# Decay attention in shares of 64 tokens: every product but the transposes as a 64x64 tile of TensorE

## The chip, the cores and the metric

One core of one Trainium2 chip runs the kernel. TensorE (PE) multiplies, and its weight loads are shown as an engine of their own (PEld); VectorE (DVE), ScalarE (ACT) and GpSimd (POOL) do the elementwise work; SyncE (SP) issues the DMAs. The metric is the device time of one launch in microseconds, the median of three runs.

## The reference

Two stages in a row. First a linear attention with decay: batch 4, 8 heads, 768 tokens, head width 64. Then a feed-forward block with softplus over all 3072 tokens, 512 to 2048 to 512 wide.

```python
gamma = 1.0 - 2.0 ** (-5.0 - np.arange(H))
for t in range(S):
    state = gamma * state + einsum('bhd,bhe->bhde', k[:, :, t], v[:, :, t])
    y[:, :, t] = (1 / sqrt(D)) * einsum('bhd,bhde->bhe', q[:, :, t], state)
x = y.transpose(0, 2, 1, 3).reshape(B * S, H * D)
h = x @ w_in                       # weights come as 64-bit floats
out = softplus(h) @ w_out
```

## The kernel before, in words

**Chunks.** The attention works on chunks of C = 128 tokens, 6 for each batch, 24 in all; `unit(m, first, pairs, when)` does chunk `m` for 8 heads (4 pairs), or, for the very first chunk, for 4 heads twice. q and v are multiplied by powers of gamma on load (`scaled`), so that a chunk needs only (1) the transposes of k and q (`tk`, `tq`, 4 each, 128x128), (2) the scores k.q of the chunk (`scores`), (3) a triangle set to zero (`mask`, an affine select of GpSimd over 128x1024 values), (4) y from the state at the start of the chunk and from the masked scores (`outputs`), and (5) the addition of the chunk's sum of k times v to the state (`update`). The state lies in `TD`, two heads to a tile, each padded with zeros to 128 rows.

**Shapes of the products.** All attention products are of full 32-bit floats, and each shows as two MATMUL records in the trace. Scores have 64 rows and 128 columns of weights, the two heads of a pair in the upper and lower half of the array (line 430). State and score shares of y have 128 rows and 64 columns of weights, 128 moving columns (lines 447 and 449). k times v has the same tile, 64 moving columns (line 453). All of them appear in the trace under line 322, the helper `mm`, with tile names by their banks: `a<-kt` is scores, `a<-ah,vn` and `a<-kt,td` are y, `a<-vn,kn` is the state. In the first chunks, buffers are lent from the weights' slots, so that `wout` or `win` stands for kt, ah or kn there. Transposes are line 417.

**The feed-forward block** runs in 6 blocks of T = 512 tokens with 16 steps each (`ffn_step`): 12 matmuls into a bank `hp` (`hp<-x,win`), softplus and a split into a rounded part `gh` and a rest `gl` on DVE, ACT and POOL (lines 515 to 519), and 12 matmuls into four banks `acc`. x itself is kept as such a pair, `xh` on ACT and `xl` on DVE (lines 461 and 462). These matmuls have 128x128 weights, 512 moving columns and one record each. During the first block the weights are fetched as 64-bit floats and turned into such pairs, too (`convert_weights`, lines 346 to 370).

**What sets the order.** All work is written down as operations with an engine, a cost, what they wait for and a due time (`when`), and `Planner.order` puts each engine's operations in one fixed order by those costs. `change` and the tables `ENTER` and `LEAVE` are the planner's prices for moving between the tile shapes R128 (feed-forward), T128 (transposes), S128 (scores) and V64 (y and state). Engines and DMA queues then run this order strictly. At the start of the program `ORDER` says which chunks and which half-width feed-forward steps (h0, h1: 256 tokens) come first; after that, chunks are added as the feed-forward steps go on, with `LEAD` and `STAGE` between due times.

## Time and profile before

| | before |
|---|---|
| median of 3 runs | 652.82 us (652.73 to 653.45) |
| the profiled execution | 651.83 us, its span 649.8 us |
| PE busy | 637.8 us (98%), 3928 matmul records |
| DVE, ACT, POOL busy | 256.9, 214.9, 239.8 us (40%, 33%, 37%) |
| TensorE's granted clock | 0.999 |

The span runs from the first to the last instruction; the execution's time has some 2 us more around it. PE's records overlap, and the end of each is modelled, so lengths of PE work are read here from the start of one row to the start of a later one.

### The profile page before, as it was taken

The page shows a single profiled execution, that of the slowest core. Times are in us where ns is not written, and L with a number is a line of the kernel's source. Part 1 is how long each engine was busy: PE and PEld are TensorE (multiplying, and loading weights), DVE is VectorE, ACT ScalarE, POOL GpSimd, SP SyncE. Part 2 cuts the span into 40 slices and gives each one's busy share as a digit, 9 for nine tenths or more (in the row PEclk, how much of TensorE's full clock was granted, in tenths as well). Part 3 has the DMA queues.
Part 4 walks back from the last instruction along what each step waited for, and adds up shares of the span by engine and source line. Part 5 has one row for each costly group of instructions (what it writes and reads, how often), then busy time and mean ns, then how long its engine had stood idle before and what let it go on. Part 6 is the DMA issues. An engine that isn't in the chain of part 4 may idle for free.

```text
span 649.8 us, 9615 instructions
## 1 busy us (share of the span) xinstructions
PE 637.8 (98%) x3928; PEld 524.7 (81%) x3928; DVE 256.9 (40%) x411; ACT 214.9 (33%) x360; POOL 239.8 (37%) x209
## 2 busy tenths in 40 slices
PE   6899999999999999999999999999999999999997
PEld 5788878888888888888888888887888888888886
DVE  5887888333232233323333324223332332322222
ACT  3776677222131222222222223122222222312221
POOL 4776777342332332232324232333223231212321
PEclk9999999999999999999999999999999999999999
DMA  9994664131102103201013201110310000100001
GB/s 230 279 310 127 212 211 125 35 80 50 33 19 53 28 17 97 49 17 33 17 32 82 66 17 30 36 33 18 98 44 5 1 1 1 65 1 0 1 1 65
DMA packets 89628, 42.58 MB, mean 66 GB/s; under 512 B 76272, under 2 KB 84464, under 8 KB 89584
## 3 DMA queue, kind: packets, MB, share of 16 engines
q1 hardware_dynamic: 89136, 41.95, 23.8%
q8 instruction: 31, 0.51, 0.3%
q14 instruction: 13, 0.11, 0.0%
q10 hardware_dynamic: 448, 0.01, 0.0%
HBM read 35.66 MB, written 6.29 MB: 65 GB/s over the span
## 4 chain that ended last, share of the span: by engine, by line
PE 97%; DMA 2%; ACT 0%; DVE 0%; issue 0%
PE acc L322 42%; PE hp L322 41%; PE a L322 11%; PE a L417 3%; DMA kn<-in_k_dram 1%; PE acc L417 0%; DMA qn<-in_q_dram 0%; ACT kt L423 0%; ACT w L554 0%; DVE qn L399 0%
## 5 line engine op out<-in xcount | busy, mean ns | idle before, releaser
L322 PE MATMUL hp<-x,win 128*128 128x512 f32 (+1 forms) x1176 | 285.3, 389 | 1.9 <-ACT x L461 1.4
L322 PEld LDWEIGHTS hp<-x,win 128*128 128x128 f32 x1176 | 214.7, 188 | 46.3 <-ACT x L461 1.5
L519 POOL TENSOR_TENSOR gl<-sp,gh 128x512 fp32r<-128x512 f32 x90 | 116.0, 1289 | 242.6 <-ACT gh L518 126.5
L322 PE MATMUL acc<-wout,gh 128*128 128x512 f32 x736 | 190.2, 394 | 0.0
L515 DVE TENSOR_SCALAR sp<-hp 128x512 uint32<-128x512 uint32 x92 | 63.6, 691 | 255.6 <-PE hp L322 172.4
L322 PEld LDWEIGHTS acc<-wout,gh 128*128 128x128 f32 x736 | 136.1, 188 | 29.7 <-issue 0.5
L516 ACT ACTIVATE sp<-sp 128x512 f32<-128x512 f32 x92 | 58.1, 631 | 271.8 <-DVE sp L515 271.6
L322 PE MATMUL acc<-wout,gl 128*128 128x512 f32 x368 | 104.7, 392 | 0.0
L517 DVE SCALAR_TENSOR_TENSOR sp<-hp,sp 128x512 f32<-128x512 f32 x92 | 63.4, 689 | 43.8 <-ACT sp L516 43.6
L322 PEld LDWEIGHTS acc<-wout,gl 128*128 128x128 f32 x368 | 68.5, 188 | 14.7 <-issue 0.2
L518 ACT CAST gh<-sp 128x512 fp32r<-128x512 f32 x90 | 55.8, 620 | 50.8 <-DVE sp L517 49.5
L399 POOL TENSOR_TENSOR vn<-vn,tabs 128x512 f32<-128x512 f32 (+1 forms) x24 | 24.2, 1009 | 57.4 <-DMA vn<-in_v_dram 57.4
L438 POOL TENSOR_SCALAR_AFFINE_SELECT ah<-ah 128x1024 f32<-128x1024 f32 x22 | 24.1, 1095 | 45.8 <-ACT ah L434 44.8
L322 PE MATMUL a<-ah,vn 128*64 128x128 f32 x352 | 33.7, 278 | 0.0
L399 POOL TENSOR_TENSOR qn<-qn,tabs 128x512 f32<-128x512 f32 x22 | 23.0, 1044 | 17.6 <-DMA qn<-in_q_dram 17.5
L322 PE MATMUL a<-kt,td 128*64 128x128 f32 x288 | 28.9, 279 | 0.0
L322 PEld LDWEIGHTS a<-kt 64*128 64x128 f32 x328 | 20.4, 187 | 7.2 <-issue 6.3
L322 PE MATMUL a<-kt 64*128 64x128 f32 x328 | 24.4, 285 | 0.0
L322 PEld LDWEIGHTS a<-ah,vn 128*64 128x64 f32 x352 | 22.4, 139 | 1.8 <-issue 0.7
L370 POOL TENSOR_TENSOR wout<-w,wout 128x512 fp32r<-128x512 f32 x16 | 20.7, 1292 | 7.2 <-ACT wout L369 7.0
L370 POOL TENSOR_TENSOR win<-w,win 128x512 fp32r<-128x512 f32 x16 | 20.7, 1291 | 6.8 <-ACT win L369 6.7
L346 ACT ACTIVATE raw<-raw 128x512 f32<-128x512 f32 x32 | 21.6, 677 | 2.9 <-DMA raw<-in_moe_w_in_dram 1.5
(99 smaller groups left out, 378.8 us busy)
## 6 DMA issues: line engine op xcount, KB each, us to landing
raw<-in_moe_w_in_dram SPq DMA_DIRECT2D x16, 512.0 KB, 6.2
raw<-in_moe_w_out_dram SPq DMA_DIRECT2D x16, 512.0 KB, 6.6
qn<-in_q_dram SPq DMA_DIRECT2D x22, 256.0 KB, 3.0
kn<-in_k_dram SPq DMA_DIRECT2D x22, 256.0 KB, 3.3
vn<-in_v_dram SPq DMA_DIRECT2D x22, 256.0 KB, 3.8
out_dram<-w SPq DMA_DIRECT2D x22, 256.0 KB, 2.6
out_dram<-win SPq DMA_DIRECT2D x2, 256.0 KB, 2.5
qn<-in_q_dram SPq DMA_DIRECT2D x2, 128.0 KB, 2.8
```

What stands on the lines that cost most here:

```text
L322: mm = lambda o, l, r, start, stop: emit(nc.tensor.matmul(o, lhsT=l, rhs=r, start=start, stop=stop))
L346: a = ACT(685, lambda word=word: emit(nc.scalar.activation(word(1).bitcast(F32), word(1).bitcast(F32), AF.Copy, scale=2.0**-112)), [ld], [ ...
L370: low_ = POOL(1300, lambda nm=nm, w=w: emit(nc.gpsimd.tensor_tensor(hl(nm, f)[:, 1], buf(w), hl(nm, f)[:, 0].bitcast(F32), op=ALU.subtract ...
L399: emit(engine.tensor_tensor(heads(held), heads(held), tabs[:, c, tab, hs].unsqueeze(2).broadcast_to([P, 2 * pairs, D]), op=ALU.mult))
L417: emit(nc.tensor.transpose(columns(tp[s], C)[:, j], heads(held)[:, 2 * j:2 * j + 2, :], ident))
L438: mask = [POOL(640 * 2, lambda: emit(nc.gpsimd.affine_select(buf(ah), buf(ah), pattern=[[0, 2], [0, pairs], [1, C]], compare_op=ALU.is_ge, ...
L515: a = DVE(vector_time(T), lambda: emit(nc.vector.tensor_scalar(U(spv()), U(bank(hp)), 0x80000000, None, op0=ALU.bitwise_or)), [lasts[-1]] ...
L516: b = ACT(640, lambda: emit(nc.scalar.activation(spv(), spv(), AF.Softplus)), [a], [sp])
L517: c = DVE(vector_time(T), lambda: emit(nc.vector.scalar_tensor_tensor(spv(), bank(hp), 0.0, spv(), op0=ALU.max, op1=ALU.add)), [b], [hp, sp])
L518: e = ACT(scalar_time(T, False), lambda: emit(nc.scalar.copy(buf(gh), spv())), [c], [sp, gh])
L519: g = POOL(1300, lambda: emit(nc.gpsimd.tensor_tensor(buf(gl), spv(), buf(gh).bitcast(F32), op=ALU.subtract)), [e], [sp, gh, gl])
```

## The change

A chunk is cut in two parts of 64 tokens, with a state of its own ahead of each (`st`, 128 x 8 x 64 values, four buffers, instead of `TD`). Every product but the transposes becomes one of 64 rows, 64 columns of weights and 64 moving columns, written in groups of four that lie in the four quarters of the array. There are two groups of work for a chunk on PE: `scores` now also makes k times v of both parts, and `outputs` makes y: a share from the state and a share from the masked scores, in separate banks. The shares of y are summed on DVE through a buffer `xs` (copies on ACT, line 497, additions on DVE, line 503, a rounding on ACT, line 506), and the rest `xl` moves from DVE to POOL (line 507). The triangle becomes a bitwise and with a 128x64 mask on DVE while the scores leave their bank (line 462); POOL's affine select goes. The copy of the transposed q moves from DVE to ACT (`QACT`). Heads are laid out as even and odd, so that q and k are loaded with two DMAs each in place of one. The numbers that steer the order are changed, the half-width steps at the start are gone, and five chunks in place of two have their q scaled on DVE.

```diff
-ORDER = ("c00", "c02", "c1", "c2", "h0", "c3", "h1")
-FETCH = 2
+ORDER = ("c00", "c01", "c1", "c2", "c3")
+FETCH = 3
...
-ENTER = {"R128": 0, "T128": 0, "S128": 188, "V64": 234}
-LEAVE = {"R128": 0, "T128": 24, "S128": 247, "V64": 127}
+ENTER = {"R128": 0, "T128": 0, "Q64": 220}
+LEAVE = {"R128": 0, "T128": 24, "Q64": 200}
...
-UNIT = 2200
+UNIT = 2600
...
-LEAD = 2700
-STAGE = 3400
+LEAD = -2000
+STAGE = 2000
...
         def scores():
-            for j in range(pairs):
-                for par in range(2):
-                    mm(columns(sc[par], C)[:, j], ktv(0)[side[par], j], ktv(1)[side[par], j], True, True)
+            for e in range(E):
+                for r in range(2):
+                    for i in range(2):
+                        mm(first_half(sc[r])[side[i], e], buf(kt)[side[r], 0, e, part(i)], buf(kt)[side[r], 1, e, part(i)], True, True)
+            for e in range(E):
+                for i in range(parts):
+                    for r in range(2):
+                        mm(second_half(sc[i])[side[r], e], quads(kn)[side[i], e // G, e % G, r], heads(vn)[side[i], 4 * (e % G) + 2 * r + e // G], True, True)
...
-        s = PE(pairs * 219, scores, ck + old(AH), [kt] + sc, when[1], "S128")
+        s = PE(2 * E * 117, scores, ck + old(AH) + [dv, *ldk], [kt, kn, vn] + sc, when[1], "Q64")
         ma = [
-            ACT(scalar_time(pairs * C), lambda: emit(nc.scalar.copy(ahv(0), columns(sc[0], C))), [s], [sc[0], ah]),
-            DVE(vector_time(pairs * C), lambda: emit(nc.vector.tensor_copy(ahv(1), columns(sc[1], C))), [s], [sc[1], ah]),
+            DVE(vector_time(E * D), lambda r=r: emit(nc.vector.tensor_tensor(buf(ah)[:, r, :E].bitcast(U32), first_half(sc[r]).bitcast(U32), mask.unsqueeze(1).broadcast_to([P, E, D]), op=ALU.bitwise_and)), [s, masked], [sc[r], ah])
+            for r in range(2)
         ]
...
+        def update(i):
+            new, old = second_half(sc[i]).rearrange("p (a g) d -> p a g d", a=2), st[i]
+            if old is not None:
+                emit(nc.vector.tensor_tensor(rows(st[i + 1]), new, rows(old), op=ALU.add))
+            else:
+                emit(nc.vector.tensor_copy(rows(st[i + 1]), new))
...
         def outputs():
...
+            for g in range(G):
+                for i in range(2):
+                    for a in range(2):
+                        for r in range(2):
+                            if st[i] is not None:
+                                mm(first_half(yp[r])[side[a], 2 * g + i], buf(st[i])[side[r], 2 * a + first + g], buf(kt)[side[r], 1, a * G + g, part(i)], True, True)
+            for g in range(G):
+                for r in range(2):
+                    for a in range(2):
+                        for i in range(2):
+                            mm(second_half(yp[i])[side[a], r * G + g], heads(vn)[side[i], 4 * g + 2 * r + a], buf(ah)[side[i], r, a * G + g], True, True)
...
-        xh = ACT(scalar_time(pairs * C), lambda: emit(nc.scalar.copy(xo(0), columns(yp, C))), [y] + xdeps, [yp])
-        xl = DVE(vector_time(pairs * C), lambda: emit(nc.vector.tensor_tensor(xo(1), columns(yp, C), xo(0).bitcast(F32), op=ALU.subtract)), [xh] + xdeps, [yp])
...
+        xb = [DVE(vector_time(E * D // (1 if c else 2)), lambda r=r: add(r), xa, [yp[r], xs]) for r in range(2)]
+        xh = ACT(scalar_time(E * C, False), lambda: emit(nc.scalar.copy(xo(0), buf(xs)[:, :E])), xb + xdeps, [xs])
+        xl = POOL(2.53 * E * C, lambda: emit(nc.gpsimd.tensor_tensor(xo(1), buf(xs)[:, :E], xo(0).bitcast(F32), op=ALU.subtract)), [xh] + xdeps, [xs])
```

In this, E is 4 for a chunk of 8 heads, G is 2, r is the half of the array by rows, and i the part of the chunk. A state's first part has no product for the first chunk of a batch, and the last chunk of a batch makes the state of one part only (`parts`).

**The order, on PE in chunk 12** (the first of the third batch), from the last products of the scores to the first ones of y. Before:

```order
L322 MATMUL a_2317<-kt_2263 128x128
L322 MATMUL a_2319<-kt_2263 128x128
L322 MATMUL hp_2330<-x_65,win_272 128x512 x12
L322 MATMUL a_2352<-ah_2334,vn_2009 64x128 x8
L322 MATMUL a_2361<-vn_2009,kn_2002 64x64 x8
```

Now:

```order
L327 MATMUL a_2792<-vn_2424,kn_2372 64x64 x2
L327 MATMUL a_2795<-vn_2424,kn_2372 64x64 x2
L327 MATMUL hp_2828<-x_65,win_553 128x512 x9
L327 MATMUL a_2850<-kt_2750,st_2843 64x64
L327 MATMUL a_2852<-kt_2750,st_2843 64x64
```

The state's products have moved ahead to the scores, and 9 matmuls of the feed-forward block lie between the two groups in place of 12.

At the start of the program the first feed-forward matmul (`hp`, `win` of step 0) stood on PE behind the y of the third chunk, at half width; now it stands behind the y of the fourth, at full width, with four transposes between.

**On POOL at the start**, from the v of the third or fourth chunk to the first `gl`. Before:

```order
L438 AFFINE_SELECT win_220<-win_220 128x1024
L370 TENSOR_TENSOR win_272<-w_267,win_272 128x512
L399 TENSOR_TENSOR qn_155<-qn_155,tabs 128x512
L370 TENSOR_TENSOR win_283<-w_279,win_283 128x512
L399 TENSOR_TENSOR vn_171<-vn_171,tabs 128x512
```

Now:

```order
L414 TENSOR_TENSOR vn_249<-vn_249,tabs 128x512
L507 TENSOR_TENSOR x_65<-xs_395,x_65 128x4x128
L375 TENSOR_TENSOR win_553<-w_516,win_553 128x512
L418 TENSOR_TENSOR qn_313<-qn_313,tabs 128x512
L507 TENSOR_TENSOR x_65<-xs_500,x_65 128x4x128
L507 TENSOR_TENSOR x_65<-xs_558,x_65 128x4x128
```

The rests of x (`x_65<-xs`) of the second to fourth chunk stand on POOL now, the last two behind the first weight's rest and a scaling of q, all ahead of the first feed-forward matmul.

**On DVE at the start**, the rows around the fourth chunk's mask. Before, in the third chunk's place:

```order
L361 SCALAR_TENSOR_TENSOR acc_264<-raw,acc_264 128x512
L471 TENSOR_TENSOR td<-acc_251,td 64x256
L366 SCALAR_TENSOR_TENSOR w_279<-raw,acc_264 128x512
L471 TENSOR_TENSOR td<-acc_251,td 64x256
L462 TENSOR_TENSOR x_65<-acc_234,x_65 128x4x128
```

Now (463 and 466 are its score banks, `xs_500` and `xs_558` the sums of y of the third and fourth chunk):

```order
L361 TENSOR_SCALAR a_502<-raw 128x512
L462 TENSOR_TENSOR ah_507<-a_463,mask 128x256
L366 SCALAR_TENSOR_TENSOR a_502<-raw,a_502 128x512
L462 TENSOR_TENSOR ah_507<-acc_466,mask 128x256
L471 TENSOR_TENSOR st_513<-a_463,st_459 128x256
L371 SCALAR_TENSOR_TENSOR w_516<-raw,a_502 128x512
L503 TENSOR_TENSOR xs_500<-acc_424,xs_500 128x2x128
L503 TENSOR_TENSOR xs_500<-acc_426,xs_500 128x2x128
L471 TENSOR_TENSOR st_561<-acc_466,st_513 128x256
L361 TENSOR_SCALAR a_566<-raw 128x512
L503 TENSOR_TENSOR xs_558<-acc_518,xs_558 128x2x128
L503 TENSOR_TENSOR xs_558<-a_520,xs_558 128x2x128
```

The mask, the states and the sums of y are now on DVE, between the steps that turn the first weights.

More of the change, by code (lines that the diff above doesn't have):

```diff
@@ L21 @@
 W = 256
-BORROW = 4
+BORROW = 5
 KT = 2
 AH = 2
-SOON = 2
-ORDER = ("c00", "c02", "c1", "c2", "h0", "c3", "h1")
-FETCH = 2
+XS = 2
+ST = 4
+QACT = 1
+SOON = 5
+ORDER = ("c00", "c01", "c1", "c2", "c3")
+FETCH = 3
 SLACK = 2.0**-17
@@ L218 @@
 RAMP = 8
-COMFORT = {"PE": 0, "ACT": 100, "DVE": 100, "POOL": 100, "SP": 0}
+COMFORT = {"PE": 0, "ACT": 0, "DVE": 0, "POOL": 0, "SP": 0}
 @with_exitstack
@@ L384, in unit @@
         if n < BORROW:
-            for held, slot in zip((kn, qn, vn, kt, ah), LATE):
+            for held, slot in zip((kn, qn, vn, kt), LATE):
                 held.among.append(slot)
-        ends = c == NC - 1
-        heads = lambda held: buf(held).rearrange("p (h d) -> p h d", d=D)[:, :2 * pairs]
-        size = 4 * P * 2 * pairs * D
+        if (m, 0) not in states:
+            states[m, 0], states[m, 1] = hold_st(), hold_st() if c < NC - 1 else None
+        st = states[m - 1, 1] if c else None, states[m, 0], states[m, 1]
@@ L395, in unit, with load_side @@
-        ldk = DMA(size, lambda: load(k, kn), [], [kn], when[0] - LOAD, 200.0)
+        def load_side(s, held, a):
+            emit(nc.sync.dma_start(heads(held)[:, a * E:(a + 1) * E], s[b, hs.start + a:hs.stop:2, c * C:(c + 1) * C, :].rearrange("h s d -> s h d")))
+        ldq = [DMA(size / 2, lambda a=a: load_side(q, qn, a), [], [qn], when[0] - LOAD, 200.0) for a in range(2)]
+        ldk = [DMA(size / 2, lambda a=a: load_side(k, kn, a), [], [kn], when[0] - LOAD, 200.0) for a in range(2)]
         ldv = DMA(size, lambda: load(v, vn), [], [vn], when[0] - LOAD, 200.0)
@@ L442, in outputs @@
-        def outputs():
-            o = [columns(yp, C)[side[par]] for par in range(2)]
-            for j in range(pairs):
-                if c:
-                    for par in range(2):
-                        mm(o[par][:, j], TD[:, par, first + j, :], ktv(1)[:, j], True, False)
-                for par in range(2):
-                    mm(o[par][:, j], heads(vn)[:, 2 * j + par, :], ahv(par)[:, j], c == 0, True)
-            if not ends:
-                for j in range(pairs):
-                    for par in range(2):
-                        mm(columns(pp, D)[side[par], j], heads(kn)[:, 2 * j + par, :], heads(vn)[:, 2 * j + par, :], True, True)
@@ L455, in unit @@
-        cost = pairs * (219 * (2 if c else 1) + 117 * (not ends))
-        state = [o for j in range(first, first + pairs) for o in stlast[j]] if c else zero
-        y = PE(cost, outputs, mask + [dv, ldk] + ck + state, [yp, vn, kn, ah, kt] + [pp] * (not ends), when[2], "V64")
-        ys.append(y)
-        xdeps = [o for j in range(first, first + pairs) for o in xread.get((i - 2, j), [])]
-        xo = lambda t: xt[:, t, off // W, js, off % W:off % W + C]
-        xh = ACT(scalar_time(pairs * C), lambda: emit(nc.scalar.copy(xo(0), columns(yp, C))), [y] + xdeps, [yp])
@@ L462, in unit @@
-        xl = DVE(vector_time(pairs * C), lambda: emit(nc.vector.tensor_tensor(xo(1), columns(yp, C), xo(0).bitcast(F32), op=ALU.subtract)), [xh] + xdeps, [yp])
-        for j in range(first, first + pairs):
-            xdone[m, j] = [xh, xl]
-        if ends:
-            return
-        def update(par):
-            new, old = columns(pp, D)[side[par]], TD[side[par], par, js]
-            if c:
-                emit(nc.vector.tensor_tensor(old, new, old, op=ALU.add))
-            else:
-                emit(nc.vector.tensor_copy(old, new))
@@ L475, in unit @@
-        up_ = [DVE(vector_time(pairs * D), lambda par=par: update(par), [y], [pp]) for par in range(2)]
-        for j in range(first, first + pairs):
-            stlast[j] = up_
+            DVE(vector_time(E * D), lambda r=r: emit(nc.vector.tensor_tensor(buf(ah)[:, r, :E].bitcast(U32), first_half(sc[r]).bitcast(U32), mask.unsqueeze(1).broadcast_to([P, E, D]), op=ALU.bitwise_and)), [s, masked], [sc[r], ah])
+            for r in range(2)
+        ]
+        rows = lambda held: buf(held).rearrange("p (a g) d -> p a g d", a=2)[:, :, first:first + G]
@@ L480, in decay_attention_then_softplus_ffn @@
+        xl = POOL(2.53 * E * C, lambda: emit(nc.gpsimd.tensor_tensor(xo(1), buf(xs)[:, :E], xo(0).bitcast(F32), op=ALU.subtract)), [xh] + xdeps, [xs])
+        for j in range(es.start, es.stop):
+            xdone[m, j] = [xh, xl]
     accs, spent = {}, {}
```

114 lines of the change are left out of this document (73 added, 41 removed).

## The prediction

> **What bounds the kernel now.** I read the shares of the engines first, then the chain that ended last, then who waits for whom, and then PE's rows in order of time. From the page, with the line of DMA's 40 slices:
>
> ```profile
> span 649.8 us, 9615 instructions
> PE 637.8 (98%) x3928; PEld 524.7 (81%) x3928; DVE 256.9 (40%) x411; ACT 214.9 (33%) x360; POOL 239.8 (37%) x209
> ...
> DMA  9994664131102103201013201110310000100001
> ...
> PE 97%; DMA 2%; ACT 0%; DVE 0%; issue 0%
> PE acc L322 42%; PE hp L322 41%; PE a L322 11%; PE a L417 3%; DMA kn<-in_k_dram 1%; PE acc L417 0%; DMA qn<-in_q_dram 0%; ACT kt L423 0%; ACT w L554 0%; DVE qn L399 0%
> ```
>
> 97% of the chain is PE, and 11% of it is `a L322`, the attention's products. From the waits:
>
> ```profile
> ACT sp L516 <- DVE sp L515: 271.6, 82, 8.3
> ...
> PE a L417 <- DVE qn L399: 3.9, 1, 3.9
> ```
>
> ACT waits 272 us for others. PE's longest wait of all is a single one of 3.9 us, at the very start. So PE is the bound, and what the change does to PE's own time counts in full, as long as the others keep up.
>
> How PE's time for a chunk is read: one chunk in the middle of the run (start, length, then the row), on the timeline of PE.
>
> ```profile
> 262.97 1.98 PE L322 MATMUL acc<-wout,gh 128*128 128x512 f32 x8
> 264.78 1.07 PE L322 MATMUL acc<-wout,gl 128*128 128x512 f32 x4
> 265.78 1.16 PE L322 MATMUL a<-kt 64*128 64x128 f32 x16
> 266.87 0.97 PE L322 MATMUL hp<-x,win 128*128 128x512 f32 x3
> 267.67 1.99 PE L322 MATMUL acc<-wout,gh 128*128 128x512 f32 x8
> 269.50 0.39 PE L322 MATMUL acc<-wout,gl 128*128 128x512 f32 x1
> 269.82 0.44 PE L322 MATMUL a<-kt,td 128*64 128x128 f32 x4
> 270.09 0.39 PE L322 MATMUL a<-ah,vn 128*64 128x128 f32 x4
> ...
> 271.62 0.63 PE L322 MATMUL a<-vn,kn 128*64 128x64 f32 x16
> 272.18 0.96 PE L322 MATMUL acc<-wout,gl 128*128 128x512 f32 x3
> 272.98 4.25 PE L322 MATMUL hp<-x,win 128*128 128x512 f32 x18
> ```
>
> A feed-forward matmul takes (264.78 - 262.97) / 8 = 0.226 us. From 264.78 to 267.67 there are 7 of them and the scores: 2.89 - 7 x 0.226 = 1.31 us for the scores. From 269.50 to 272.98 there are 4 and y with the state: 3.48 - 4 x 0.226 = 2.58 us.
>
> **The price inside.** From 270.09 to 271.62 stand seven rows of 4 records: 14 pairs in 1.53 us, 0.109 us for two at once. The 16 records `a<-vn,kn` span 0.63 us; one alone lasts 0.224 us by this row of the groups:
>
> ```profile
> L322 PE MATMUL a<-vn,kn 128*64 128x64 f32 x264 | 11.1, 224 | 0.0
> ```
>
> So eight pairs need (0.63 - 0.22) / 7 = 0.058 us each. That a pair runs at once is seen in the scores of an early chunk, where the two halves of the array write two banks, `a` and `acc`:
>
> ```profile
> 12.48 0.37 PE L322 MATMUL a<-wout 64*128 64x128 f32 x1
> 12.49 0.37 PE L322 MATMUL acc<-wout 64*128 64x128 f32 x1
> 12.70 0.27 PE L322 MATMUL a<-wout 64*128 64x128 f32 x1
> ```
>
> Scores are 8 pairs, 0.87 us, so 0.44 of their 1.31 us is the move into and out of that tile shape. y is 16 pairs of 0.109 and 8 of 0.058, 2.21 us, so 0.37 us is its move.
>
> **The change on PE, in the steady part.** A product of 64 rows, 64 columns and 64 moving columns is again two records. Pairs in two row halves (scores) and pairs in two column halves (y) each run at once; a group of four uses both splits together, each half with the load that it has now. I take 0.058 us for a group of four, the price of a 64-column pair. The other end is that four need two such pairs, 0.116 us. I take the first, since the rows 12.48 and 12.49 begin within 0.01 us of each other, so that four begin within 0.04 us, less than 0.058.
>
> One rule of the Trainium skill speaks against it. "TensorE: Matmul & The Clock Gate", section "Wait — 56ns, not 53.3ns?", says that start-to-start never falls under about 25 ns, however small the matmul; then four records would need 0.100 us, and the sum below would be a loss of 4 to 9 us in place of a gain. The row above with 0.01 us between two starts does not agree with it for one pair; as a mean, 0.058 / 2 = 0.029 us for a record is the lowest that this trace has, so no row here shows a mean under 25 ns.
>
> Counts for a chunk: scores 32 records, both states 32, y from state 32, y from scores 32, in all 32 groups, 16 in each of two blocks of 0.93 us. For the move into and out of the new shape the nearest rows are 0.37 and 0.44; I take 0.44, the one that splits rows, for each block. Ends: 0.37, or 0.81 if the two splits add.
>
> - Chunk in the middle of a batch: 1.31 + 2.58 = 3.89 before, 2 x (0.93 + 0.44) = 2.74 after: 1.15 saved.
> - First chunk of a batch (no state yet; y before 8 + 8 pairs, 1.71; after 12 groups): 3.02 before, 1.37 + 1.14 = 2.51 after: 0.51 saved.
> - Last (no state to make; y before 2.11): 3.42 before, 1.14 + 1.37 = 2.51 after: 0.91 saved.
>
> From the fifth chunk on there are 13, 3 and 4 of these: 14.95 + 1.53 + 3.64 = 20.1 us. With 0.37 for a move it is 22.9.
>
> **The other engines.** Durations by shape, from the groups:
>
> ```profile
> L519 POOL TENSOR_TENSOR gl<-sp,gh 128x512 fp32r<-128x512 f32 x90 | 116.0, 1289 | 242.6 <-ACT gh L518 126.5 <-issue 103.8 <-PE a L417 6.3
> L515 DVE TENSOR_SCALAR sp<-hp 128x512 uint32<-128x512 uint32 x92 | 63.6, 691 | 255.6 <-PE hp L322 172.4 <-POOL gl L519 81.2 <-issue 1.9
> L518 ACT CAST gh<-sp 128x512 fp32r<-128x512 f32 x90 | 55.8, 620 | 50.8 <-DVE sp L517 49.5
> L438 POOL TENSOR_SCALAR_AFFINE_SELECT ah<-ah 128x1024 f32<-128x1024 f32 x22 | 24.1, 1095 | 45.8 <-ACT ah L434 44.8 <-DVE ah L435 0.9
> L399 POOL TENSOR_TENSOR vn<-vn,tabs 128x512 f32<-128x512 f32 x22 | 23.0, 1045 | 53.6 <-DMA vn<-in_v_dram 53.6
> L423 ACT COPY kt<-a 128x512 f32<-128x512 f32 x21 | 12.3, 587 | 23.5 <-PE a L417 23.1
> L471 DVE TENSOR_TENSOR td<-a,td 64x256 f32<-64x256 f32 x26 | 10.9, 419 | 19.4 <-PE a L322 19.2
> L462 DVE TENSOR_TENSOR x<-a,x 128x256 fp32r<-128x256 f32 x2 | 0.8, 424 | 0.1
> L461 ACT CAST x<-a 128x256 fp32r<-128x256 f32 x2 | 0.7, 372 | 1.4 <-PE a L322 1.4
> ```
>
> For a chunk, DVE loses three copies of 0.69 and two state additions of 0.42 and gains two masks, two states and two sums of y, six of 0.42 (the bitwise and is priced as the addition of the same size): 2.91 to 2.54 us. ACT loses three of 0.59 and gains two of 0.59, two of 0.37 and one of 0.62: 1.76 to 2.54. POOL loses the select of 1.10 and gains 1.29 for `xl`: 3.18 to 3.38. SP issues 5 loads in place of 3; DMA's slices stand at 4 tenths or lower from the seventh on. All of this costs nothing in the steady part, since the idle times in the rows of lines 519 and 515 (243 and 256 us) cover it.
>
> A new wait stands between the two blocks: y waits for both masks and the first state, three DVE operations, 1.27 us, and some 0.2 us of handing over. In chunk 12, nine matmuls stand between the blocks, 2.03 us, in place of twelve with POOL's select behind the copies. So 0.5 us is spare; one softplus operation of 0.69 in the way on DVE would cost PE 0.2 us. I put this at 0 to 2 us over all chunks. Then the next thing to be late is `xl`: y to x is now 0.74 + 0.84 + 0.62 + 1.29 = 3.5 us over ACT, DVE, ACT and POOL; it matters only where a block's first feed-forward matmul is near, and the last chunk that it needs lies well ahead there.
>
> **The start.** First feed-forward matmul at 19.27; by 43.45, PE has done four chunks, the fifth's transposes and scores, and feed-forward work of 48 full matmuls (48 of half width, and 24 full ones):
>
> ```profile
> 4.00:8.00 4.00, 3.54 (x17) 2.23 (x18) 2.21 (x9) 0.81 (x3) 1.29 (x3) 1.00 1.02 226
> 8.00:12.00 4.00, 4.00 (x40) 3.37 (x42) 2.43 (x7) 1.61 (x4) 2.87 (x6) 1.00 1.08 209
> ...
> 3.86 0.66 PE L417 MATMUL a<-ident,qn 128*128 128x128 f32 x2 [3.86 <-DVE qn L399]
> ...
> 19.27 0.38 PE L322 MATMUL hp<-x,win 128*128 128x256 f32 x1 [1.36 <-ACT x L461]
> ...
> 25.08 0.60 PE L417 MATMUL acc<-ident,kn 128*128 128x128 f32 x4
> ...
> 26.04 0.44 PE L322 MATMUL a<-kt,td 128*64 128x128 f32 x4
> ...
> 43.45 0.97 PE L322 MATMUL hp<-x,win 128*128 128x512 f32 x3
> ```
>
> (The last column of the first two rows is GB/s in that stretch; the one before it, DMA's share, is full.) Now the first feed-forward matmul waits for all four chunks. Their q, k and v are 12 x 262 kB = 3.15 MB, at 218 GB/s 14.4 us, from about 2.7 (first product at 3.86, after a scaling of 0.42 and handing over): the fourth chunk's v is there at 17.1. Then one after another: POOL's scaling 1.05, scores 1.37, masks and state 1.27, y 1.37, ACT 0.74, DVE 0.84, ACT 0.62, POOL 1.29: 25.7, if no queue stands in the way. In the order, DVE has four steps for the first weights (0.69 each) and four others of 0.42 between, and POOL has the weight's rest, a scaling and the third chunk's `xl` (1.29 + 1.05 + 1.29) ahead of the fourth's. POOL's weight step can begin at about 23.4 (fourth chunk's scores at 20.0; DVE's two masks, two weight steps and a state to 22.6; ACT's rounding to 23.3), and four POOL operations of 4.9 us end at 28.3. I take 28.5; ends 25.7 and 32 (fourteen handings-over of 0.25 us more). From there 48 x 0.226 + 0.96 for eight transposes (25.08 to 26.04) + 1.37 = 13.2 us: 41.7 in place of 43.45, 1.8 saved, with ends 4.6 and -1.7. PE's work on the four chunks is shorter by more than that; the rest of it turns into waiting, as the half-width steps that filled PE are gone.
>
> **Sum.** 20.1 + 1.8 = 21.9. The profiled execution took 651.8 us; it should take 629.9. The median shown is 1.0 above it, so 630.9, said as 631. Likeliest case's range: 652.8 - 22.9 - 4.6 = 625.3 to 652.8 - 20.1 + 1.7 + 2 = 636.4.
>
> **Rivals.**
> - *Four do not run at once* (the slower side). Records come no closer on average than 0.029 us, the lowest mean in the trace, or a row and a column split exclude each other: 0.116 us for a group. For it: no row shows more than two at once. Against: the start distance of 0.01 us, and that neither split slows its pair. There are 736 groups in all (2944 records), 612 behind the start: 35 to 43 us more, 666 to 674. It decides from 21.9 / 612 = 0.036 us above the 0.058, that is 0.094 us for a group. The 25 ns of the page named above would lie just past this point, at 656 to 662 by its figure.
> - *DVE becomes the wait.* If masks and state come 0.4 to 0.7 us late at y in each of 20 chunks, since sums of y and softplus steps stand ahead of them on DVE, 8 to 14 us of the gain go: 639 to 645. Against: DVE has less to do than before, and 0.5 us is spare.
> - *The moves between shapes cost 0.81 us*, both splits added: 40 x 0.37 = 14.8 us go, 646.
>
> **How the numbers follow.** 0.74 for my forecast, 0.12 for the first rival, 0.10 for the second, 0.04 for the third. The range from 625 to 643 holds nearly all of the first and the better half of the second: 8 in 10. About 0.2% (1.3 us) is what a measurement of this kernel can tell from no change. Faster by more: 0.74 + 0.10 + most of the third = 0.87; the same 0.01; slower 0.12.
>
> **What the profile after will show.** Right: 64x64 rows of 64 records that last 0.93 us from the first to the last start, 1.37 us with their moves; PE at 98% from 30 us on; the first feed-forward matmul between 26 and 32 us; no PE wait on line 462 or 471 (masks, states) worth more than 2 us in total. Wrong: 64 records in 1.6 us or more; a wait of y for DVE in each chunk; a first `hp` after 32 us, or `hp` waiting for line 507 (`xl`) at the beginning of a block.

## The result, and the profile after

The changed kernel takes 635.45 us (median of 4 runs, 635.13 to 635.99) beside 653.13 us for the kernel before in the same session (4 runs, 652.73 to 653.48): a ratio of 0.973, 95% interval 0.9713 to 0.9747. That is 17.7 us less; 21.9 were forecast. The profiled execution took 635.32 us, its span 633.6; it is 16.5 us under the profiled execution of the kernel before (651.83), which was itself a little under that kernel's median. Two executions of one variant below ran at a granted clock of 0.66 and 0.56 and took 880 and 1026 us; its time leaves them out.

The page of the changed kernel, first its sums and the granted clock in 40 slices, then the line of the instruction queue and the chain that ended last:

```profile
span 633.6 us, 12824 instructions
PE 615.8 (97%) x5440; PEld 502.9 (79%) x5440; DVE 243.4 (38%) x443; ACT 227.9 (36%) x410; POOL 241.8 (38%) x207
...
PEclk9879999999999999999999999999999999999999
...
q8 instruction: 43, 0.70, 0.5%
...
PE 93%; DMA 2%; DVE 1%; issue 1%; ACT 1%; SPq 1%; POOL 1%; ACTq 0%; DVEq 0%
PE acc L327 42%; PE hp L327 41%; PE a L327 7%; PE a L435 3%; DMA raw<-in_moe_w_in_dram 1%; POOL x L507 1%; DMA wout<-in_q_dram 0%; SPq L405 0%; DMA qn<-in_q_dram 0%; PE acc L435 0%; DMA kn<-in_k_dram 0%; DVE a L366 0%; DVE w L371 0%; DVE sp L549 0%; SPq L344 0%
```

PE's busy time fell by 22.0 us (637.8 to 615.8), the span by 16.2. PE still carries the end, but 7% of the chain now belongs to others where it was 3%, and the clock falls to 0.8 and 0.7 in the second and third slices, where it was full. The instruction queue brought 43 packets of 16 kB instead of 31. So the work on PE shrank as meant, and something was lost at the start.

**The steady part.** PE's timeline in the middle of the run, around the scores of one chunk (start, length, row) and around the y of another:

```profile
262.36 1.07 PE L327 MATMUL acc<-wout,gl 128*128 128x512 f32 x4
263.27 0.84 PE L327 MATMUL hp<-x,win 128*128 128x512 f32 x3
264.04 0.69 PE L327 MATMUL a<-kt,st 64*64 64x64 f32 x32
264.56 0.65 PE L327 MATMUL a<-ah,vn 64*64 64x64 f32 x32
265.13 2.11 PE L327 MATMUL acc<-wout,gh 128*128 128x512 f32 x8
267.08 1.07 PE L327 MATMUL acc<-wout,gl 128*128 128x512 f32 x4
...
284.55 1.98 PE L327 MATMUL acc<-wout,gh 128*128 128x512 f32 x8
286.36 1.07 PE L327 MATMUL acc<-wout,gl 128*128 128x512 f32 x4
287.36 0.69 PE L327 MATMUL a<-kt 64*64 64x64 f32 x32
287.88 0.65 PE L327 MATMUL a<-vn,kn 64*64 64x64 f32 x32
288.45 0.97 PE L327 MATMUL hp<-x,win 128*128 128x512 f32 x3
289.26 1.08 PE L327 MATMUL acc<-wout,gh 128*128 128x512 f32 x4
```

With 0.227 us for a feed-forward matmul, 284.55 to 289.26 holds 15 of them (3.40) and the scores with the states: 1.31 us. 262.36 to 267.08 holds 15 again and y: 1.32 us. Taken from the starts of PE's instructions in the whole trace, all 33 blocks of 64 records cost 1.29 us. None of these rows has a wait.

That four run at once is seen in an early chunk, where the buffers' names differ:

```profile
16.04 0.22 PE L327 MATMUL acc<-wout,st 64*64 64x64 f32 x1
16.05 0.22 PE L327 MATMUL a<-wout,st 64*64 64x64 f32 x1
16.05 0.22 PE L327 MATMUL acc<-wout,st 64*64 64x64 f32 x1
16.06 0.22 PE L327 MATMUL a<-wout,st 64*64 64x64 f32 x1
16.10 0.22 PE L327 MATMUL acc<-wout,st 64*64 64x64 f32 x1
```

Four begin within 0.02 us, and the next four 0.06 us after the first. In the steady part the groups of four follow each other at 0.058 us, so that the mean distance of two records is 0.0145 us.

**The start.** PE's timeline, the rows with a wait (in brackets: how long and for whom) and the first feed-forward matmuls, then the windows in which the clock is low:

```profile
20.75 0.51 PE L327 MATMUL acc<-kt,st 64*64 64x64 f32 x19 [0.91 <-issue]
...
24.58 0.24 PE L327 MATMUL a<-kt,st 64*64 64x64 f32 x1 [1.85 <-DVE st L471]
...
27.64 0.21 PE L327 MATMUL acc<-kt,st 64*64 64x64 f32 x1 [2.72 <-issue]
...
30.95 1.09 PE L435 MATMUL a<-ident,qn 128*128 128x128 f32 x4 [1.84 <-ACT raw L351]
31.69 0.78 PE L327 MATMUL hp<-x,win 128*128 128x512 f32 x1
33.01 0.79 PE L327 MATMUL hp<-x,win 128*128 128x512 f32 x1 [0.54 <-POOL x L507]
...
53.24 0.97 PE L327 MATMUL hp<-x,win 128*128 128x512 f32 x3
```

```profile
24.00:28.00 4.00, 0.70 (x32) 0.60 (x35) 2.62 (x7) 1.17 (x2) 1.27 (x1) 1.00 1.12 345
28.00:32.00 4.00, 2.16 (x51) 1.96 (x42) 2.02 (x4) 2.81 (x6) 2.62 (x3) 0.51 1.10 243
32.00:36.00 4.00, 3.46 (x9) 2.41 (x8) 3.33 (x7) 3.53 (x8) 3.01 (x3) 0.50 0.89 218
36.00:40.00 4.00, 4.00 (x16) 3.16 (x16) 1.40 (x3) 1.91 (x4) 3.73 (x4) 0.71 1.12 318
```

By 53.24, PE has done 69 full matmuls, the fifth chunk's scores and four transposes of the sixth. The point of the prediction (48 full matmuls) is therefore 53.24 - 21 x 0.226 - 0.44 = 48.05 us, where the kernel before was at 43.45. The start lost 4.6 us instead of saving 1.8. With the 16.2 us by which the span fell, the rest of the program saved 20.8.

Two of the waits are for nothing that the profile shows (`<-issue`): in the middle of a row of products, all of whose data is there, PE stands still for 0.9 and 2.7 us. Counted from the program's beginning, these are PE's instructions 705 and 961 (loads, matmuls and PE's own steps on semaphores together), 256 apart, and the 16 kB packets of the instruction queue start at 12.45, 18.47, 24.80 and 30.10 us.

### The profile page after: what moved, and what is told of

Same layout as the page of the kernel before. It is cut to its first block, busy times and chain, and to the rows that moved or that the text cites. A ratio compares the mean times of both kernels' runs of the same rounds, so it can differ in the third digit from the quotient of the medians.

```text
span 633.6 us, 12824 instructions
## 1 busy us (share of the span) xinstructions
PE 615.8 (97%) x5440; PEld 502.9 (79%) x5440; DVE 243.4 (38%) x443; ACT 227.9 (36%) x410; POOL 241.8 (38%) x207
## 2 busy tenths in 40 slices
DMA packets 90442, 42.79 MB, mean 68 GB/s; under 512 B 77073, under 2 KB 85265, under 8 KB 90385
## 3 DMA queue, kind: packets, MB, share of 16 engines
q1 hardware_dynamic: 89936, 41.95, 23.8%
## 4 chain that ended last, share of the span: by engine, by line
PE 93%; DMA 2%; DVE 1%; issue 1%; ACT 1%; SPq 1%; POOL 1%; ACTq 0%; DVEq 0%
PE acc L327 42%; PE hp L327 41%; PE a L327 7%; PE a L435 3%; DMA raw<-in_moe_w_in_dram 1%; POOL x L507 1%; DMA wout<-in_q_dram 0%; SPq L405 0%; DMA qn<-in_q_dram 0%; PE acc L435 0%; DMA kn<-in_k_dram 0%; DVE a L366 0%; DVE w L371 0%; DVE sp L549 0%; SPq L344 0%
## 5 line engine op out<-in xcount | busy, mean ns | idle before, releaser
L327 PE MATMUL hp<-x,win 128*128 128x512 f32 x1152 | 289.2, 396 | 0.7 <-POOL x L507 0.5
L327 PE MATMUL acc<-wout,gl 128*128 128x512 f32 x368 | 102.5, 390 | 0.0
L507 POOL TENSOR_TENSOR x<-xs,x 128x512 fp32r<-128x512 f32 (+1 forms) x25 | 31.5, 1263 | 65.5 <-ACT x L506 65.5
L497 ACT COPY xs<-a 128x256 f32<-128x256 f32 (+1 forms) x45 | 14.5, 369 | 53.2 <-PE a L327 53.2
L503 DVE TENSOR_TENSOR xs<-a,xs 128x256 f32<-128x256 f32 (+2 forms) x45 | 16.1, 388 | 39.6 <-ACT xs L497 39.5
L442 ACT COPY kt<-a 128x512 f32<-128x512 f32 (+1 forms) x21 | 12.1, 576 | 48.1 <-PE a L435 47.9
L462 DVE TENSOR_TENSOR ah<-a,mask 128x256 uint32<-128x256 uint32 x42 | 16.0, 420 | 22.4 <-PE a L327 22.2
L418 POOL TENSOR_TENSOR qn<-qn,tabs 128x512 f32<-128x512 f32 x20 | 21.1, 1054 | 8.4 <-DMA qn<-in_q_dram 7.4
L375 POOL TENSOR_TENSOR wout<-w,wout 128x512 fp32r<-128x512 f32 x16 | 20.8, 1302 | 9.0 <-ACT wout L374 9.0
L366 DVE SCALAR_TENSOR_TENSOR a<-raw,a 128x512 uint32<-128x512 uint32 x32 | 21.5, 690 | 0.9 <-DMA kn<-in_k_dram 0.3
```

Of the source, the lines that this page charges most:

```text
L327: mm = lambda o, l, r, start, stop: emit(nc.tensor.matmul(o, lhsT=l, rhs=r, start=start, stop=stop))
L366: lambda word=word, wp=wp: emit(nc.vector.scalar_tensor_tensor(bits(wp), word(1), 0x80000000, bits(wp), op0=ALU.bitwise_and, op1=ALU.bitwi ...
L375: low_ = POOL(1300, lambda nm=nm, w=w: emit(nc.gpsimd.tensor_tensor(hl(nm, f)[:, 1], buf(w), hl(nm, f)[:, 0].bitcast(F32), op=ALU.subtract ...
L418: emit(engine.tensor_tensor(all_, all_, by, op=ALU.mult))
L507: xl = POOL(2.53 * E * C, lambda: emit(nc.gpsimd.tensor_tensor(xo(1), buf(xs)[:, :E], xo(0).bitcast(F32), op=ALU.subtract)), [xh] + xdeps, ...
```

## The experiments

The theory after the result was that PE waits for its own instructions. A packet of 16 kB holds 256 of them (11011 instructions came in 43 packets), the changed kernel has 11011 on PE where the kernel before had 7953, and while DMA is nearly full (its share is 0.94 to 1.12 in each 4 us from 8 to 32 us) the packets come some 6 us apart, in which PE gets 256 instructions and no more. Rivals were the order at the start, the low clock, the conversion of the weights, and the loads of q, k and v.

**The order of before at the start.**

```diff
-ORDER = ("c00", "c01", "c1", "c2", "c3")
+ORDER = ("c00", "c01", "c1", "c2", "h0", "c3", "h1")
```

> The changed kernel with the order of the start from before: half-width feed-forward steps after the third and the fourth chunk again, all else as changed. Theory: the start lost some 6 us against the forecast because PE had nothing to do between 21.8 and 31.7 us (two stops in its own instruction stream, 1.1 and 2.9 us, then the full-width step's wait for all four chunks, then half the clock from 27.7 to 38.0 us). Half-width steps fill that: 4 to 6 us less than the changed kernel, 629.5 to 631.5 us, and a granted clock of 1.00 all through. Rival: the stops in the instruction stream set the start whatever the order is, and only move: at most 1.5 us less, 634 to 636 us.

It took 638.62 us, ratio 0.9777 (0.9758 to 0.9795), 3 us more than the change as it is, and outside both expectations. The first weights' loads now stand ahead of the fourth chunk's, and PE waits for the third chunk's state, up to 4.8 us at once:

```profile
23.67 0.44 PE L327 MATMUL a<-kt,st 64*64 64x64 f32 x2 [4.81 <-DVE st L471]
```

So putting the half-width steps back does not win the loss back. As it also moves the weights' loads, it does not show what the steps alone are worth.

**Instructions moved by 64, and the clock kept up.** The first kernel has 16 small products more at the very start of PE, so that another instruction stands at each 256th place; the second also has 28 transposes behind the fourth chunk's y, so that PE is not idle there.

```diff
+            mm(bank(spare)[:, :D], ident, ident[:, :D], True, True)
...
+    PE(60 * 2 * MORE, more, [], [spare], -1e6, "T128")            # MORE = 16
...
+                for _ in range(WARM):                              # WARM = 28, second kernel only
+                    emit(nc.tensor.transpose(bank(warm[0])[:, :C], ident, ident))
```

> The changed kernel with 16 small products more at the very beginning, while PE waits for the first q: 64 PE instructions more (32 matmul records, 32 weight loads), written to an unused bank. Theory: the two stops come where PE's instructions run out of a fetched page of 256 (they stood at PE instructions 705 and 961 of the stream, exactly 256 apart), so they come 64 instructions earlier in the work now: the second one in the fourth chunk's scores instead of its y, where the wait for the mask follows anyway and hides about 2 us of it. First feed-forward matmul 1.5 to 2.5 us earlier, 633 to 634.5 us. Rival: the stops belong to those matmuls (a wait that the trace does not name): they stay between the same matmuls of y, and the time stays within 0.5 us of the changed kernel.

> The kernel of the shifted page, and 28 transposes of the identity more into an unused bank, just behind the fourth chunk's y, where PE waits for the sums of y (3.1 us of work that nothing needs). Theory: the clock falls to half when PE has stood for some 3 us, and that costs about 2 us (ten full matmuls at 0.427 in place of 0.227 us); with PE kept at work the clock stays at 1.00, and the time is 1.5 to 2.5 us under the shifted page alone, 631 to 633 us. Rival: what sets the start is the chain over DVE, ACT and POOL, and PE's slow matmuls hide in it: no difference of more than 0.5 us from the shifted page alone.

The stops stayed at places 705 and 961 of PE's stream (1.5 and 3.2 us long in the first kernel), though other products stand there now. At the first stop it is a product for the state (the first kernel's timeline).

```profile
22.28 0.27 PE L328 MATMUL a<-vn,kn 64*64 64x64 f32 x1 [1.51 <-issue]
```

The first took 639.6 us, ratio 0.9791 (0.9778 to 0.9804), outside both expectations: the small products hold back the first transposes by some 4 us, so its time says nothing of the instructions. The second has 0.5 of the clock for 6.8 us where the first has it for 13.7, and took the same, 639.38 us, ratio 0.979 (0.9777 to 0.9804). Its timeline, then that of the first:

```profile
38.17 2.98 PE L329 MATMUL hp<-x,win 128*128 128x512 f32 x12
42.38 0.66 PE L442 MATMUL a<-ident,kn 128*128 128x128 f32 x4 [1.23 <-DVE w L373]
42.79 3.00 PE L329 MATMUL hp<-x,win 128*128 128x512 f32 x12
```

```profile
37.42 5.06 PE L328 MATMUL hp<-x,win 128*128 128x512 f32 x11 [0.71 <-POOL x L508]
...
42.98 3.09 PE L328 MATMUL hp<-x,win 128*128 128x512 f32 x12
```

At full clock the first twelve matmuls are done early and PE then waits 1.23 us for the next weight, so that the second twelve begin at 42.79 in place of 42.98. The low clock costs next to nothing here (0.2 us), since the weights' conversion on DVE is no earlier. In the change as it is, without the 16 products, this was not tried.

**Each quarter of the array by itself.** The loops are turned, so that each quarter's products stand in a row instead of alternating between the four.

```diff
-            for e in range(E):
-                for r in range(2):
-                    for i in range(2):
+            for r in range(2):
+                for i in range(2):
+                    for e in range(E):
                         mm(first_half(sc[r])[side[i], e], buf(kt)[side[r], 0, e, part(i)], buf(kt)[side[r], 1, e, part(i)], True, True)
...
```

> The changed kernel with the loops of both blocks turned round, so that all products of one quarter of the array stand together, then those of the next (8 records of one quarter in a row and more, in place of 2). Same instructions, same data. Theory: PE looks ahead in its stream only so far, so that the order in groups of four is what makes four run at once; a block of 64 records then takes up to 64 x 0.058 = 3.7 us in place of 0.93, up to 2.8 us more for each of 46 blocks: over 30 us more, 665 us or above. Rival: each quarter has its own queue deep enough for the block's 16 records: no change, 635 to 636 us.

693.85 us, ratio 1.0626 (1.0612 to 1.0641): 58 us more than with the quarters in turn, and 41 more than the kernel before. A block of 64 records costs 2.81 us in all 33 places, where it cost 1.29; the rows of one y:

```profile
291.76 0.84 PE L327 MATMUL hp<-x,win 128*128 128x512 f32 x3
292.53 1.36 PE L327 MATMUL a<-kt,st 64*64 64x64 f32 x29
...
293.91 1.31 PE L327 MATMUL a<-ah,vn 64*64 64x64 f32 x29
295.15 2.11 PE L327 MATMUL acc<-wout,gh 128*128 128x512 f32 x8
```

The same products in another order lose the whole gain and more. It is the order in groups of four that makes them run at once.

**More and fewer instructions in the first chunks.** In one kernel the third chunk's scores are made four times (192 instructions more); in the other, products of the first four chunks that lie side by side are written as one, with the weights of the first alone (some 450 instructions fewer; these chunks' values are not the reference's).

```diff
+            for _ in range(AGAIN if n == 3 else 1):                # AGAIN = 4
```

```diff
+                        if few:                                    # the first four chunks
+                            if e % 2 == 0:
+                                mm(first_half(sc[r])[side[i], e:e + 2], buf(kt)[side[r], 0, e, part(i)], buf(kt)[side[r], 1, e:e + 2, part(i)], True, True)
+                            continue
...
```

> The changed kernel, but the third chunk issues its score products four times (same result): 192 PE instructions more (96 matmul records, 96 weight loads) in the start, and 24 groups of four, 1.4 us, of PE work. Theory: at the start PE runs out of instructions: a page of 256 comes every 5 to 7 us while the loads of q, k, v and weights keep all DMA engines full, and PE's stream of the first four chunks (1070 instructions to the end of the fourth chunk's y) uses them up sooner. 192 instructions more are 0.75 of a page, 4 to 5 us: first feed-forward matmuls at 35.5 to 38 us in place of 31.7 and 33.0, 639 to 641 us; stops again at PE instructions 705 and 961 of the stream. Rival: the start is set by DMA, DVE, ACT and POOL; PE has 6 us of idle time there, which hides 1.4 us of work: 635 to 636.5 us.

> The changed kernel, but in the first four chunks two neighbouring products with 64 moving columns are issued as one with 128 (the first one's weights serve both, so that the numbers of these chunks are not the reference's): half the records and weight loads there, the same PE time. Theory (PE's instruction pages): the end of the fourth chunk's y comes at PE instruction 620 or so, before the stop at 705 and well before 961; both stops are gone from the chunks, first full feed-forward step 2.5 to 4 us earlier, and the time with it, 631.5 to 633 us. Rival: something else holds the fourth chunk's y (its mask or state on DVE): 635 to 636 us.

The first took 640.05 us, ratio 0.9793 (0.9776 to 0.9811), 4.6 us more. The 96 records more would run in 1.4 us at 0.0145 each; 192 instructions at 6.2 us for 256 make 4.65. The packets start at 12.16, 18.58, 24.75 and 30.40 us, nearly where they did, and the stops are at 705 and 961 again, now 2.2 and 3.0 us long:

```profile
20.94 0.27 PE L328 MATMUL a<-kt 64*64 64x64 f32 x1 [2.15 <-issue]
...
27.41 0.81 PE L328 MATMUL acc<-ah,vn 64*64 64x64 f32 x19 [3.01 <-issue]
```

The second took 633.71 us, ratio 0.9702 (0.9689 to 0.9715), 1.7 us less than the change as it is, between theory and rival; the first feed-forward matmul comes at 30.04 in place of 31.69. No stop for `issue` is left; the packets start at 13.02, 23.8 and 43.5. But PE then waits for data (its timeline, and DVE's row behind it):

```profile
24.94 0.29 PE L328 MATMUL a<-kt,st 64*64 64x128 f32 x1 [3.25 <-DVE st L482]
...
29.27 1.12 PE L437 MATMUL a<-ident,qn 128*128 128x128 f32 x4 [3.15 <-POOL qn L420]
...
31.75 4.79 PE L328 MATMUL hp<-x,win 128*128 128x512 f32 x11 [0.93 <-POOL x L526]
```

```profile
22.52 0.69 DVE L362 TENSOR_SCALAR a<-raw 128x512 uint32<-128x512 uint32 x1 [2.25 <-DMA raw<-in_moe_w_in_dram]
```

DVE stands 2.25 us at the first weight's step, which waits for its load, with the fourth chunk's masks and states in line behind it. The instructions were one limit, the data another that lies 1.7 us below it.

**The mask alone, in the kernel before.** POOL's select and the two copies are replaced by two bitwise ands on DVE.

```diff
-            ACT(..., lambda: emit(nc.scalar.copy(ahv(0), columns(sc[0], C))), ...),
-            DVE(..., lambda: emit(nc.vector.tensor_copy(ahv(1), columns(sc[1], C))), ...),
+            DVE(..., lambda par=par: emit(nc.vector.tensor_tensor(ahv(par).bitcast(U32), columns(sc[par], C).bitcast(U32), bits..., op=ALU.bitwise_and)), ...)
+            for par in range(2)
```

> The kernel before with one part of the change alone: the triangle as a bitwise and with a 128x128 mask on DVE while the scores leave their banks, in place of a copy on ACT, a copy on DVE and POOL's select of 1.1 us. Theory: in the steady part PE never waits for the mask, so this is worth nothing there, and at the start at most the 1.0 us that PE waited for the third chunk's select: 651.5 to 653.5 us. Rival: a shorter way from scores to y lets the order close up: 648 to 651 us.

654.96 us, ratio 1.0026 (1.0016 to 1.0035): 1.6 us more, a little outside both. The blocks cost what they did (scores 1.29, y with state 2.56 us). At the start, though, PE waits 1.48 and 1.60 us at the first feed-forward matmuls, where the kernel before waits 1.36 and 0.55, then 1.14 us for a mask on DVE (line 437), for which the kernel before has no wait, and the clock is at 0.5 for 3.4 us. The timeline of this kernel, then the row of the kernel before that stands against the second wait:

```profile
19.10 0.38 PE L325 MATMUL hp<-x,win 128*128 128x256 f32 x1 [1.48 <-ACT win L372]
21.09 0.51 PE L325 MATMUL hp<-x,win 128*128 128x256 f32 x2 [1.60 <-DVE x L462]
...
35.88 0.44 PE L325 MATMUL acc<-kt,td 128*64 128x128 f32 x4 [1.14 <-DVE ah L437]
```

```profile
20.20 0.50 PE L322 MATMUL hp<-x,win 128*128 128x256 f32 x2 [0.55 <-DVE x L462]
```

So the mask is worth nothing by itself in the steady part, and work moved to DVE at the start has a price there.

**How far ahead weights are loaded.**

```diff
-FETCH = 3
+FETCH = 2
```

> The changed kernel with FETCH = 2 as before the change: one feed-forward step's weights less are loaded without waiting at the start, and the planner orders the first block anew. Theory (PE's instruction pages wait behind loads in full DMA queues): fewer loads in flight shorten the stop at PE instruction 961 from 2.9 us to 1 to 2.5 us; if the rest of the order is as good, 632 to 635 us. Rival: q, k and v fill the queues anyway, the stops stay as long as they are, and the time is set by the new order, either way within 3 us of 635.5.

636.35 us, ratio 0.975 (0.9728 to 0.9773): no better. Packets at 12.03, 18.81, 24.98 and 30.20, a stop at 961 of 1.6 us, the first feed-forward matmul at 33.07.

**The loads at the start.** Three kernels: the k of the first three chunks issued by ACT instead of SP; the first part of `w_in` loaded ahead of the fourth chunk instead of behind it; both.

```diff
-            emit(nc.sync.dma_start(heads(held)[:, a * E:(a + 1) * E], ...
+            emit((nc.scalar if s is k and n < SPLIT else nc.sync).dma_start(heads(held)[:, a * E:(a + 1) * E], ...   # SPLIT = 4
```

```diff
-            ld = DMA(8 * P * n, load, free + [pace[-2 * FETCH]] if len(pace) >= 2 * FETCH else [], [raw])
+            ld = DMA(8 * P * n, load, free + [pace[-2 * FETCH]] if len(pace) >= 2 * FETCH else [], [raw], 14000.0 if (nm, f) == ("win", 0) else None)
```

> The two DMAs of k of the first three chunks (eight issues, the first chunk has two halves) are issued by ACT instead of SP; nothing else is changed. Theory: at the start the loads stand in line on SP. In the changed kernel it issues 20 half loads of about 0.5 us each before the first weight load, which leaves at 16.06 us where it left at 8.27 in the kernel before, and POOL gets the fourth chunk's v at 20.68, not at 17.1 as the prediction had it. With 4 us less on SP the fourth v is there at 18 to 19, the first weight at 19 to 20, the first full feed-forward matmul at 29 to 30 in place of 31.7, and the time is 632 to 634. Rival: the DMA engines are full from 8 us on (share 1.0 and more), so an earlier issue lands no earlier: 635 to 636, first feed-forward within 0.5 us of 31.7.

> Only the load of the first part of w_in is issued ahead of the fourth chunk's loads in place of behind them. Theory: the first feed-forward matmul is late because the first weight lands at 21.8 us and its steps on DVE stand among the masks and sums of y; the weight 4 us earlier brings the first feed-forward matmul to 29 to 30.5 and the time to 633 to 634.5. Rival: DMA is full, so the 0.5 MB only change places with the fourth chunk's, which comes 2.3 us later; its y and x then end last, the first feed-forward matmul comes at 31.5 to 33.5, and the time is 635 to 637.5.

> The two edits together: k of the first three chunks issued by ACT, and the first part of w_in loaded ahead of the fourth chunk. If SP's line and the weight's place both hold the start, 631 to 633, with the first feed-forward matmul at 27.5 to 29; if the DMA engines' share is what counts, 635 to 637; if only the line on SP counts, as with k on ACT alone (632 to 634).

637.45 us, ratio 0.9763 (0.9742 to 0.9785); 635.74 us, ratio 0.9742 (0.9721 to 0.9762); 637.63 us, ratio 0.9768 (0.9749 to 0.9786). None is better. With ACT as the second issuer the times lie about 2 us above the change as it is and above what was expected either way, though with a wide spread (635.63 to 639.47 and 636.62 to 638.71, against 635.13 to 635.99). Its loads stand in line with its copies, the last at 11.48 us, and SP's own issues take as long as before (2.4 us for the two of the fourth q); the first weight load leaves at 16.27 where it left at 16.06. With the weight ahead of the fourth chunk its step is at 20.34 instead of 21.90, and POOL gets the fourth v at 22.31 instead of 20.68. The first feed-forward matmul is at 33.13, 33.91 and 34.74. So taking issues off SP brings the loads no earlier, and the weight's place by itself changes nothing. What a shorter line on SP would bring is not shown, since it did not get shorter.

**The loads in larger pieces.** q, k and v of the first four chunks come as whole rows of 0.5 to 2 kB, as many bytes as before but not the values that the chunks need.

```diff
+            if n < WHOLE:                                          # WHOLE = 5
+                emit(nc.sync.dma_start(buf(held)[:, a * 2 * G * D:(a + 1) * 2 * G * D], run(s, 2 * G * D, n * P * 512 + a * P * 2 * G * D)))
+                return
...
```

> The q, k and v of the first four chunks are read as the same number of bytes from one stretch of the tensor, so that each row of a buffer is one piece of 0.5 to 2 kB instead of 4 to 8 pieces of 256 bytes; these are not the values of the heads and tokens that the chunk needs, so that the numbers are not the reference's, and the work of all engines, the order and the number of DMAs stay. Theory: the start is held by the rate at which DMA moves q, k and v (some 207 to 232 GB/s in small pieces, share 1.0, against 350 to 400 GB/s where the weights come in later). With larger pieces the fourth v comes at 15 to 17 us in place of 20.68 and the first weight at 16 to 18 in place of 21.8, PE's instructions are fetched sooner, the first full feed-forward matmul starts at 25 to 28, and the time is 629 to 631.5. Rival: it is the chain from engine to engine (POOL's scaling, scores, mask, state, y, four steps to x, with the weight's steps between them) that sets the start; the time is 633.5 to 636 and the first feed-forward matmul stays within 2 us of 31.7.

636.2 us (634.35 to 636.65), ratio 0.9729 (0.9705 to 0.9753): no gain. The loads do come sooner: 275 GB/s from 8 to 16 us instead of 232 and 207, the first weight load leaves SP at 12.75, POOL gets the fourth v at 17.88 instead of 20.68, and the first weight's step on DVE, at 19.90, waits for no DMA. DMA's share is 0.94 and 0.90 there in place of 1.07 and 1.06. But the packets of instructions start at 13.81, 19.84, 25.81 and 29.90, 6 us apart as before, and now it is PE that stands, and DVE that waits for PE:

```profile
16.13 0.21 PE L328 MATMUL acc<-wout,st 64*64 64x64 f32 x1 [1.30 <-issue]
...
22.45 0.58 PE L328 MATMUL acc<-kt,st 64*64 64x64 f32 x24 [2.86 <-issue]
```

```profile
25.49 0.42 DVE L472 TENSOR_TENSOR ah<-a,mask 128x256 uint32<-128x256 uint32 x1 [4.92 <-PE acc L328]
```

This is the mirror of the kernel with fewer instructions. Two limits lie close together at the start, PE's instructions and the data (with the weight's steps in DVE's line). Taking away the first brings 1.7 us, taking away the second alone brings nothing. Both at once was not run, and no run shows what sets the 6 us between packets.

## Why the prediction was right or wrong

**A group of four at 0.058 us** was right: 33 blocks alike, and the four that begin within 0.02 us. The rival that four do not run at once, and the 0.116 us of the other end, are out. So is, for these tiles, the rule of the Trainium skill that it weighed ("TensorE: Matmul & The Clock Gate", section "Wait — 56ns, not 53.3ns?", a floor of about 25 ns from start to start): here the mean is 14.5 ns. The kernel with each quarter by itself shows what the group of four rests on: at 2.81 us for a block, (2.81 - 0.36) / 64 is 0.038 us a record.

**The move** was put at 0.44 us a block and measured 1.29 - 0.93 = 0.36, just under the lower end of 0.37. The two splits do not add, and the third rival (0.81) is out.

**The savings in a chunk** were forecast as 1.15, 0.51 and 0.91 us (middle, first, last). By the blocks of both traces they are 1.29 + 2.56 - 2 x 1.29 = 1.27; 1.29 + 1.68 - 1.29 - 1.06 = 0.62; 1.29 + 2.09 - 1.28 - 1.29 = 0.81. The last is smaller since the block of its scores is 1.28 us where 1.14 was forecast: its state, of one part only, fills two quarters, so that these 16 records run as pairs and not in groups of four. The sum is 13 x 1.27 + 3 x 0.62 + 4 x 0.81 = 21.6 us; forecast 20.1, measured by the ends 20.8. Two short waits in the feed-forward block, at 96.0 (0.72 us) and 122.2 us (0.32), make up about that difference.

**The other engines cost nothing in the steady part**: right but for these two waits, which are for ACT's rounding (line 550) and DVE's softplus step (line 549). No chunk's y waits for DVE, and the second rival is out. The whole list of PE's waits for a mask or a state holds one of 1.9 us, that at 24.58 in the start. The 0 to 2 us set aside for the new wait were not used after the start.

**The start** is the step that failed: `1.8 saved, with ends 4.6 and -1.7`, measured 4.6 lost, a miss of 6.4 us and outside its ends. The first feed-forward matmul came at 31.69, inside the 25.7 to 32 but 3.2 us behind the 28.5. The other 3.2 us were lost behind it: 48.05 - 31.69 = 16.4 us where 13.2 were forecast, since the second matmul waited for `xl` (the sign named for a wrong forecast, `hp` waiting for line 507) and the weights paced the next. The forecast also put all 48 matmuls at 0.226 us; from 33.01 to 37.87 eleven of them took 0.44 us each at half the clock, but in the kernel kept at full clock PE then waited for the next weight instead. Three things were left out of its sum.
- PE's instructions. PE's work on four chunks was taken as free to start when its data was there. In the trace it stands 0.9 and 2.7 us for its instructions, which are 38% more; kernels with 192 more and some 450 fewer took 4.6 us more and 1.7 less.
- The fourth v was put at 17.1 us, with 218 GB/s from 2.7 us on; POOL has it at 20.68. DMA moved only 160 GB/s from 4 to 8 us and 207 to 232 from 8 to 20, and SP issued this load at 15.56.
- The first weight was taken to be there. Its load leaves SP at 16.06 behind four chunks (at 8.27 in the kernel before), and its step on DVE waits for it until 21.90, with the fourth chunk's masks behind.

What is shown of this: the instructions alone hold 1.7 us, and another limit, the data, stands right behind them. The earlier data alone, the weight's place alone and, in the shifted kernel, the clock alone bring nothing, and in each of these another wait took the place of the one removed. That the second and third point together with the first make up the 6.4 us is argued, not shown. From the 73rd feed-forward matmul to the last, each kernel with the same order needs the same time: 575.4 us in the change, 575.6 with fewer instructions, 575.5 with more, 575.4 with larger pieces. So their difference is made before.

**The total** came 4.5 us above the 631, inside the likeliest case's range, with the mechanism right on PE and the start as the term that was wrong. That it still lies inside is partly luck. With the start's 4.6 us lost in the prediction's own sum, the range would have ended at 652.8 - 20.1 + 4.6 + 2 = 639.3 and its middle stood near 637.3. The rest of the program saved 0.7 us more than the 20.1, the 2 us set aside were not needed, and the median lay 0.1 us above its profiled execution, not 1.0.

## What to carry to other kernels

Small fp32 products gain from being cut to 64x64 only when the four quarters of the array take turns in program order: the same products quarter by quarter cost 58 us more here. Such products multiply PE's instructions, so count those (256 to a packet of 16 kB). The stops here came while DMA was busy most of the time; that this is why the packets came late is not shown. A wait for `issue` in the middle of a row of products, at a fixed distance of 256 instructions, is what a starved instruction queue looks like. At a start that several limits share, removing one shows only the distance to the next, so forecast the start by the latest of all chains, the order of the loads among them.

## What the runs showed of the hardware

- **Instructions are fetched while the program runs, and it can be seen.** In the change's start the packets of 16 kB begin 6.0, 6.3 and 5.3 us apart, and 4.1 to 6.8 us apart in the three variants above in which PE stops for them and whose packets are listed; after the start PE uses them up more slowly, and no stop follows. The Trainium skill says the same of the packets of 256 instructions ("Runtime: NRT & Kernel Launch", section "Instruction fetch mechanics"), and that the cost of crossing from one to the next is mostly hidden. In these starts, with DMA's share between 0.7 and 1.2, it was not: up to 3.2 us a crossing (the kernel with 16 small products more).
- **A mean of 14.5 ns between matmul records** in groups of four 64x64 tiles, 0.058 us for four with 64 moving columns, and 0.36 us for the move into and out of that shape.
- **The granted clock** fell to 0.5 at 28.07 us, after PE had been busy only 0.70 of 4 us (window 24 to 28), and came back 10.2 us later. In the kernel with 28 transposes more it came back after 6.8 us, in the one with the mask alone after 3.4, and in the one with larger pieces only after 17.1.
